# One instruction or four for each background matmul: the form chosen by the pace at which TensorE's code is fetched

## The chip, the cores and the metric

The kernel runs on one core of one Trainium2 chip. The metric is the time of one execution on the device in microseconds (us); lower is better. Below, PE is TensorE, ACT is ScalarE, DVE is VectorE, POOL is GpSimd, and SP is the engine that issues the DMAs.

## The reference

One transformer layer in bfloat16 on 2048 tokens of width 1024, with 32 heads of 32 and a hidden width of 3584:

```python
x = A_x                                        # 1 x 2048 x 1024
qkv = layernorm(x) @ wqkv                      # 1024 x 3072
p = softmax(q @ k.T * 32 ** -0.5)              # per head, 2048 x 2048
h = x + (p @ v) @ wo                           # 1024 x 1024
g = gelu(layernorm(h) @ w1 + b1)               # 1024 x 3584
out = h + g @ w2 + b2                          # 3584 x 1024
```

## The kernel before

The whole layer is one static program. A planner in Python (`Graph`) holds every step as a task with an engine, an estimated duration `occ`, a latency and its dependencies. `schedule` (line 113) plays the five engines forward in time and so fixes each engine's order; `assign` (line 255) turns the dependencies between engines into semaphore waits; `emit` (line 348) writes each engine's list out. Nothing is decided at run time: each engine runs its list in order and stops at a wait that has not come true.

**Attention** goes by queries: eight blocks of 256 queries, and in each block eight groups of four heads. A round takes 256 keys of one group. Its score matmuls (line 838) use the 128x128 array as four row strips, one head to a strip (mode "row"), and fill two units of PSUM; ACT takes the exponential of each unit (line 850). Then come the weighted sums of V (line 879) and the sums of the exponentials (line 918, with DVE adding pairs first at line 894); both use the array as four column strips of 32 (mode "col"). The last two groups of the last query blocks are done in halves of 128 queries. There are three PSUM units for scores, so PE can be at most one and a half rounds ahead of ACT.

**Background work** is everything else that is a matmul: the projections to Q, K and V, the output projection, and the two matmuls of the feed-forward part of earlier query blocks. `pick_pe` (line 1327) prefers scores whenever their PSUM is free, then weighted sums, then background, so background matmuls fill the gaps between attention's groups in PE's list. The planner charges 0.104 us each time PE goes from one mode to another.

A background matmul computes a 128-wide result block from 128 rows. In `mm` (line 588) it gets two forms, the same arithmetic into the same PSUM bank: a list of four matmuls of 128x32, one for each column strip, mode "col" (issued at line 596), or `whole`, one matmul of 128x128, mode "full" (issued at line 599). Each matmul that the kernel writes becomes two instructions of PE, a weight load and the matmul, and each wait of a task beyond the first is an instruction of its own. Some tasks have the one form only (line 602, and transposes at line 669): they are mode "full" from the start and `whole` is not set.

All background tasks with two forms are planned as "col". After planning, `merge_tiles` (line 240) changes some of them to "full": in a run of consecutive "col" tasks, a stretch of background work at its end becomes "full" if the run holds nothing else, or if the stretch takes at least 3.0 us.

Of the kernel before, what the change touches and what calls it, by code (L numbers as in the profile page):

```python
# [16 lines left out]

BULK = {1: 3, 2: 2}
UNIT = 1 << 19


class Buf:
# [42 lines left out]
class Graph:  # L65
# [47 lines left out]
    def schedule(self, pick_pe, pool, switch=0.104, dma_rate=280.0, dma_lat=2.1, dma_issue=0.06):  # L113
# [14 lines left out]
        def behind(t):  # L128
            k = BULK[t.prio] - t.bytes // UNIT
            for b in reversed(bulk):  # L130
                k -= b.bytes // UNIT
                if k < 0:
                    return b
            return None
# [20 lines left out]
        while n < total:  # L155
# [5 lines left out]
            for e in self.ENGS:  # L161
                while free[e] <= now + 1e-9:
# [8 lines left out]
                    else:  # L171
                        go = rd
                        if e == E.SP:
                            go = []
                            for x in rd:
                                b = behind(x) if x.bytes >= UNIT and x.prio in BULK else None
                                if b is None or b.done <= now + 1e-9:
# [27 lines left out]
                    if e == E.SP:  # L205
                        if t.bytes >= UNIT and t.prio in BULK:
                            b = behind(t)
# [10 lines left out]
                        s0 = max(state["dma"], start + 0.9)  # L218
                        state["dma"] = s0 + t.bytes / (330.0 if t.bytes >= UNIT and t.prio in BULK else dma_rate) / 1e3
                        t.done = max(state["dma"], s0) + dma_lat - 0.9  # L220
# [16 lines left out]
        return seqs  # L237


    def merge_tiles(self):  # L240

        run = []
        for t in self.seqs[E.PE] + [None]:
            if t is not None and t.mode == "col":
                run.append(t)
                continue
            k = len(run)
            while k and run[k - 1].whole is not None:
                k -= 1
            if k == 0 or sum(x.occ for x in run[k:]) >= 3.0:  # L250
                for x in run[k:]:
                    x.fns, x.mode = [x.whole], "full"
            run = []

    def assign(self, flows, lane_flows):

# [102 lines left out]
def build_kernel(nc, A_x, A_wqkv, A_wo, B_w1, B_b1, B_w2, B_b2, out):  # L359
    _, S, D = A_x.shape  # L360
# [16 lines left out]
    gr = Graph(N_LANES)  # L377
# [795 lines left out]
    for hc in range(8):  # L1173
# [7 lines left out]
        for k, r in [(k, hc) for k in range(min(hc, NLJ))] + ([(hc, r) for r in range(hc + 1)] if hc < NLJ else []):  # L1181
            n = 8 * k + r
            s = NR + 15 if n == 0 else n - 1 if n < 9 else n
# [174 lines left out]

    num = {t: i for i, t in enumerate(gr.tasks)}
    gr.schedule(pick_pe, pool_banks)  # L1360
    gr.merge_tiles()

    sems = {e: nc.alloc_semaphore(f"f_{e.name}") for e in (E.PE, E.Activation, E.DVE, E.Pool)}
    lanes = [nc.alloc_semaphore(f"f_lane{i}") for i in range(N_LANES)]
    gr.assign(sems, lanes)
    finals = [(("L", t.lane), t.value) for t in gr.seqs[E.SP][-40:]]

    with nc.Block() as block:
# [24 lines left out]
def bass_sequential_preLN__softmax_full_mha__dense_activation_gelu__prompt_kernel(  # L1393
    nc: bass.Bass,
    A_x: bass.AP,
    A_wqkv: bass.AP,
    A_wo: bass.AP,
    B_x: bass.AP,
    B_w1: bass.AP,
    B_b1: bass.AP,  # L1400
    B_w2: bass.AP,
    B_b2: bass.AP,
    out: bass.AP,
):
    build_kernel(nc, A_x, A_wqkv, A_wo, B_w1, B_b1, B_w2, B_b2, out)
# [28 lines left out]
```

## Time and profile before

| What | Value |
|---|---|
| Median of 3 timed runs | 1076.15 us (1075.17 to 1078.43) |
| Profiled execution's own time | 1076.72 us |
| Its span, first to last instruction | 1075.1 us |
| Granted TensorE clock, mean over the span | 0.998 |
| ACT busy | 1007.9 us (94%) |
| PE busy (ends of matmuls are modelled) | 1043.5 us (97%) |
| Matmuls on PE | 17,978 |
| DMA traffic, mean | 179 GB/s |

The profile is of one execution, and its span is 1.6 us shorter than that execution's own time. "Idle before" and "waits" name what ended an engine's idle time; "issue" there means that nothing which the profile shows was waited for. PEld is the weight load, which runs beside PE's matmuls. q8 is the DMA queue by which PE's instructions come, and PEclk is the granted share of TensorE's clock.

### The profile page before, as it was taken

The numbers are of one execution on the slowest core, as the hardware profiler recorded it, in microseconds if no ns is written. First come the engines' busy times: TensorE is split into PE (matmuls) and PEld (weight loads), VectorE is DVE, ScalarE is ACT, GpSimd is POOL, SyncE is SP. The second block draws the span as 40 slices with busy tenths as digits, with TensorE's granted clock in tenths as the row PEclk, the third lists the DMA queues.
The fourth block names the chain that finished last, engine by engine and source line by source line (L and its number), as shares of the span: only waits on it lengthen the run. The fifth ranks groups of instructions, "written<-read, shape, count | busy, mean of one in ns | idle before, by whom it ended". The sixth has DMA issues, their size and how long they took to land.

```text
span 1075.1 us, 39701 instructions
## 1 busy us (share of the span) xinstructions
PE 1043.5 (97%) x17978; PEld 605.1 (56%) x17978; DVE 783.2 (73%) x1521; ACT 1007.9 (94%) x1117; POOL 49.3 (5%) x110
## 2 busy tenths in 40 slices
PE   8999999999999999999999999999999899998998
PEld 6576555554445744664574456447546644663575
DVE  8766666566677995797599569749978967997560
ACT  4999999999999999999999989999999999999732
POOL 4200000000000010001001000100010000000000
PEclk9999999999999999999999999999999999999999
DMA  8470544335665546746554664657377453677730
GB/s 233 114 185 21 176 134 119 120 119 163 208 195 161 194 155 205 268 165 204 204 206 160 208 232 162 207 186 229 137 229 250 145 191 118 231 256 262 244 131 16
DMA packets 130649, 192.04 MB, mean 179 GB/s; under 512 B 47024, under 2 KB 95024, under 8 KB 127920
## 3 DMA queue, kind: packets, MB, share of 16 engines
q1 hardware_dynamic: 130480, 189.50, 54.2%
q8 instruction: 141, 2.31, 0.8%
q14 instruction: 28, 0.23, 0.1%
HBM read 175.32 MB, written 26.21 MB: 187 GB/s over the span
## 4 chain that ended last, share of the span: by engine, by line
PE 50%; ACT 41%; DMA 3%; DVE 3%; issue 1%; POOL 1%; SPq 0%; DVEq 0%
ACT PT L850 37%; PE ps L599 24%; PE ps L838 8%; PE ps L596 6%; PE ps L879 6%; PE ps L602 3%; PE ps L918 3%; ACT uu L1069 2%; ACT PX L850 2%; DMA a_w2r<-w_blocks 1%; DVE PS L894 1%; DMA w1b<-w_blocks 1%; DMA q_scratch<-lq 1%; DVE st L648 1%; DMA xrb<-in_A_x_dram 0%
## 5 line engine op out<-in xcount | busy, mean ns | idle before, releaser
L850 ACT ACTIVATE PT<-ps 128x1024 bf16<-128x1024 f32 x992 | 925.3, 1188 | 12.1 <-PE ps L838 11.7
L894 DVE TENSOR_TENSOR PS<-PT 128x1024 bf16<-128x1024 bf16 x427 | 280.1, 684 | 77.2 <-PE ps L918 40.3
L838 PE MATMUL ps<-QT,KT 32*128 32x256 bf16 (+1 forms) x4352 | 204.3, 266 | 10.4 <-ACT PT L850 6.8
L879 PE MATMUL ps<-PT,V 128*32 128x256 bf16 (+1 forms) x4224 | 160.4, 267 | 1.8 <-ACT PT L850 1.8
L838 PEld LDWEIGHTS ps<-QT,KT 32*128 32x128 bf16 x4352 | 64.6, 92 | 166.4 <-ACT PT L850 152.6
L599 PE MATMUL ps<-a_w2r,gT 128*128 128x512 bf16 x609 | 152.2, 381 | 3.2 <-DVE gT L1071 1.5
L599 PE MATMUL ps<-hnT,a_w1r 128*128 128x256 bf16 x1165 | 144.3, 275 | 0.6 <-DVE hnT L678 0.4
L599 PEld LDWEIGHTS ps<-hnT,a_w1r 128*128 128x128 bf16 x1165 | 107.8, 98 | 31.7 <-issue 18.2
L879 PEld LDWEIGHTS ps<-PT,V 128*32 128x32 bf16 x4224 | 101.3, 97 | 25.0 <-issue 7.6
L918 PE MATMUL ps<-PS,ones 128*32 128x256 bf16 (+1 forms) x1692 | 108.6, 268 | 1.0 <-DVE PS L894 0.8
L599 PEld LDWEIGHTS ps<-a_w2r,gT 128*128 128x128 bf16 x609 | 52.1, 98 | 73.7 <-issue 16.6
L1051 DVE TENSOR_TENSOR gT<-ps,b1f 128x512 bf16<-128x512 f32 x98 | 67.3, 687 | 22.1 <-PE ps L596 10.9
L599 PE MATMUL ps<-xnT,Wall 128*128 128x512 bf16 (+1 forms) x364 | 79.9, 355 | 0.4 <-ACT xnT L676 0.3
L1069 ACT ACTIVATE uu<-uu 128x1024 bf16<-128x1024 bf16 (+1 forms) x53 | 62.5, 1199 | 13.4 <-DVE uu L1068 13.4
L1124 DVE SCALAR_TENSOR_TENSOR hch<-ps,hch 128x512 bf16<-128x512 f32 x32 | 21.9, 685 | 71.2 <-PE ps L599 37.5
L596 PE MATMUL ps<-hnT,a_w1r 128*32 128x256 bf16 x1612 | 61.1, 274 | 6.3 <-issue 5.8
L599 PE MATMUL ps<-wov,OT 128*128 128x512 bf16 x224 | 56.0, 380 | 0.0
L918 PEld LDWEIGHTS ps<-PS,ones 128*32 128x32 bf16 x1692 | 42.9, 96 | 18.5 <-issue 6.3
L653 POOL CAST mvb<-mv 128x2 bf16<-128x2 f32 (+1 forms) x25 | 6.4, 254 | 984.6 <-DVE mv L650 984.6
L596 PE MATMUL ps<-a_w2r,gT 128*32 128x512 bf16 x700 | 50.2, 381 | 0.0
L599 PEld LDWEIGHTS ps<-xnT,Wall 128*128 128x128 bf16 x364 | 31.2, 97 | 33.0 <-issue 10.4
L596 PEld LDWEIGHTS ps<-hnT,a_w1r 128*32 128x32 bf16 x1612 | 40.8, 96 | 15.6 <-issue 13.9
(102 smaller groups left out, 992.6 us busy)
## 6 DMA issues: line engine op xcount, KB each, us to landing
a_w2r<-w_blocks SPq DMA_DIRECT2D x105, 512.0 KB, 4.6
a_w1r<-w_blocks SPq DMA_DIRECT2D x98, 512.0 KB, 3.9
wov<-wo_blocks SPq DMA_DIRECT2D x16, 1024.0 KB, 4.8
w_blocks<-in_B_w_dram SPq DMA_DIRECT2D x28, 512.0 KB, 3.9
w1b<-w_blocks SPq DMA_DIRECT2D x14, 512.0 KB, 4.2
Wall<-in_A_wqkv_dram SPq DMA_DIRECT2D x17, 256.0 KB, 4.5
xrb<-in_A_x_dram SPq DMA_DIRECT2D x16, 256.0 KB, 4.9
a_w1r<-in_A_wqkv_dram SPq DMA_DIRECT2D x8, 512.0 KB, 5.0
```

Of the source, the lines that this page charges most:

```text
L596: fns.append(lambda p, j=j: p.matmul(psum[32 * j:32 * j + 32, bi(bank), c0:c1], lhsT[:, 32 * j:32 * j + 32], rhs, start=start, stop=stop, ...
L599: t.whole = lambda p: p.matmul(psum[:, bi(bank), c0:c1], lhsT, rhs, start=start, stop=stop, skip_group_check=True)
L602: t = pe(lambda p: p.matmul(psum[:, bi(bank), c0:c1], lhsT, rhs, start=start, stop=stop), occ, reads=reads, writes=[bb(bank)], mode="full" ...
L648: dve(lambda v, c=c, k=k, x_ap=x_ap: v.bn_stats(st_l[:, i + k, 6 * c:6 * c + 6], x_ap[:, 512 * c:512 * c + 512]), 0.595, reads=B_x if isin ...
L838: return p.matmul(psum[:, 2 * us[h // 2] + h % 2, n * i:n * i + n], KT[32 * h:32 * h + 32, g, k0:k0 + P], QT[32 * h:32 * h + 32, qs, q0:q0 ...
L850: act(lambda a, u=u, k=k: a.activation(PTs[s][:, k, :, :], psum[:, 2 * u:2 * u + 2, :], ACT.Exp, bias=0.0, scale=SCALE), 1024, reads=[B_ps ...
L879: fns.append(lambda p, i=i, h=h: p.matmul(psum[32 * h:32 * h + 32, bi(bank), 0:nq], V[:, g, kt * r + i, 32 * h:32 * h + 32], PTs[s][:, h / ...
L894: dve(lambda v: v.tensor_tensor(PS[:, n, :, :], pairs[:, :, 0:256], pairs[:, :, 256:512], ALU.add), c_dve(1024, 2), reads=B_PTs[s], writes ...
L918: fns.append(lambda p, h=h, rhs=rhs, i=i: p.matmul(psum[32 * h:32 * h + 32, bi(bank), 256:256 + nq], ones32[:, :], rhs, start=False, stop= ...
L1051: t = dve(lambda v: v.tensor_tensor(g[:, fc:fc + nf, :], psum[:, bi(bank), :].rearrange("p (f c) -> p f c", f=nf), b1f[:, fc:fc + nf].unsq ...
L1069: act(lambda a: a.activation(w, w, ACT.Tanh, bias=0.0, scale=KT2), m, reads=[B_uu[i]], writes=[B_uu[i]], prio=-1)
L1124: drop(dve(lambda v: v.scalar_tensor_tensor(hch[:, hs, c], psum[:, bi(bank), :], half, hch[:, hs, c], ALU.mult, ALU.add), c_dve_ps(512), r ...
```

## The change

`merge_tiles` is replaced by `choose_forms`, which runs after `assign` instead of before it, when each task's waits are known. PE's list is cut into parts: stretches of background tasks with two forms, and stretches of everything else. For each stretch with two forms it picks one form for the whole stretch. To choose, it walks through PE's list counting instruction places (two for each matmul, one for each wait beyond the first), each with the planner's time. Places 192, 448, 704 and so on, every 256, are marks. If less time passes between two marks than a fetch takes, the difference is added to a price; `FETCH` lists ten fetch times, and the price is the mean over them. A stretch in full form pays 0.104 more for each side on which it meets other "col" work. The walk keeps the cheapest way to each position within a block (at most about 700 states) and takes the cheapest at the end.

The planner, the order of every engine and the waits are not touched.

```diff
+FETCH = (2.05, 2.55, 2.75, 3.0, 3.2, 3.45, 3.75, 4.15, 4.65, 5.75)
...
-    def merge_tiles(self):
-
+    def choose_forms(self, block=256, at=192, switch=0.104, weight=1.0):
+
+        parts = []
         run = []
         for t in self.seqs[E.PE] + [None]:
             if t is not None and t.mode == "col":
                 run.append(t)
                 continue
-            k = len(run)
-            while k and run[k - 1].whole is not None:
-                k -= 1
-            if k == 0 or sum(x.occ for x in run[k:]) >= 3.0:
-                for x in run[k:]:
-                    x.fns, x.mode = [x.whole], "full"
+            k = 0
+            while k < len(run):
+                n = k
+                while n < len(run) and (run[n].whole is None) == (run[k].whole is None):
+                    n += 1
+                ends = (k > 0) + (n < len(run))
+                parts.append((run[k:n], None if run[k].whole is None else switch * ends))
+                k = n
             run = []
+            if t is not None:
+                parts.append(([t], None))
+
+        def walk(ts, full):
+            marks, c = [], 0
+            for t in ts:
+                n = 1 if full else len(t.fns)
+                s = t.done - t.occ - t.lat
+                for w in t.waits[1:]:
+                    marks.append(s)
+                for i in range(n):
+                    marks += [s + t.occ * i / n, s + t.occ * (i + 1) / n]
+            return marks
+
+        states = {(2, 0): (0.0, 0.0, None)}
+        for p, (ts, extra) in enumerate(parts):
+            forms = [(False, 0.0)] if extra is None else [(True, extra), (False, 0.0)]
+            forms = [(f, x, walk(ts, f)) for f, x in forms]
+            new = {}
+            for (c, _), (price, t0, back) in states.items():
+                for f, x, marks in forms:
+                    y, s0 = price + x, t0
+                    k = (at - c) % block
+                    while k < len(marks):
+                        y += weight * sum(max(0.0, l - marks[k] + s0) for l in FETCH) / len(FETCH)
+                        s0 = marks[k]
+                        k += block
...
+        price, _, back = min(states.values(), key=lambda x: x[0])
+        self.fetch_price = price
+        while back is not None:
+            p, f, back = back
+            if f:
+                for t in parts[p][0]:
+                    t.fns, t.mode = [t.whole], "full"
...
     gr.schedule(pick_pe, pool_banks)
-    gr.merge_tiles()
...
     gr.assign(sems, lanes)
+    gr.choose_forms()
```

## Prediction, made before the changed kernel was run

> **What bounds the kernel now.** The page comes first.
>
> ```profile
> PE 1043.5 (97%) x17978; PEld 605.1 (56%) x17978; DVE 783.2 (73%) x1521; ACT 1007.9 (94%) x1117; POOL 49.3 (5%) x110
> q8 instruction: 141, 2.31, 0.8%
> PE 50%; ACT 41%; DMA 3%; DVE 3%; issue 1%; POOL 1%; SPq 0%; DVEq 0%
> ```
>
> ACT, with 992 exponentials, and PE share the chain. The q8 line matters here. PE has 17,978 weight loads, as many matmuls, and 138 others (waits that need an instruction of their own, two drains): 36,094. The 2.31 MB of q8 are 64 bytes for each, its 141 packets of 16 KB hold 256 each, 36,096 in all. So q8 is PE's own code, fetched while it runs.
>
> Second view, the waits: those of ACT from 80 us, where all is under way, to 990 us, near attention's end; those of ACT from 600 to 660 and from 850 to 885 us; and PE's weight loads (PEld) from 80 to 1005 us:
>
> ```profile
> ACT PT L850 <- PE ps L838: 7.3, 8, 2.4
> ...
> ACT PT L850 <- PE ps L838: 4.6, 3, 2.4
> ...
> ACT PT L850 <- PE ps L838: 2.0, 3, 1.0
> ...
> PEld ps L838 <- ACT PT L850: 146.7, 442, 1.9
> ```
>
> Over 910 us ACT waits 7.3 us for the scores (L838), 4.6 of it between 600 and 660 and 2.0 between 850 and 885. Elsewhere it is full, and in 442 of 512 groups the scores' weight loads wait for ACT: here a microsecond of ACT idleness is a microsecond of the end. Third view, the chain in order of time around the largest idle time, with ACT's rows of the timeline and the granted clock below it:
>
> ```profile
> 629.92 0.44 PE ps L596 x16
> 630.35 2.61 issue
> 632.97 0.51 PE ps L596 x12
> 633.48 0.41 PE ps L838 x8
> 633.89 2.89 PE ps L599 x13
> ...
> 637.23 1.53 PE ps L599 x13
> 638.76 0.33 PE ps L838 x8
> ...
> 643.56 1.53 PE ps L596 x52
> ...
> 645.97 0.33 PE ps L838 x8
> ```
>
> ```profile
> 633.93 1.94 ACT L850 ACTIVATE PT<-ps 128x1024 bf16<-128x1024 f32 x2 [2.40 <-PE ps L838]
> 637.29 2.87 ACT L850 ACTIVATE PT<-ps 128x1024 bf16<-128x1024 f32 x3 [1.42 <-PE ps L838]
> ```
>
> ```profile
> 634.00:635.00 1.00, 1.00 (x6) 0.74 (x5) 0.00 (x0) 1.00 (x2) 0.00 (x0) 0.50 0.27 102
> 635.00:636.00 1.00, 1.00 (x7) 0.69 (x6) 0.26 (x1) 0.87 (x1) 0.00 (x0) 0.50 0.02 8
> 636.00:637.00 1.00, 1.00 (x12) 0.37 (x10) 1.00 (x3) 0.00 (x0) 0.00 (x0) 0.50 0.26 98
> ```
>
> PE stops for 2.61 us inside a run of narrow matmuls, waiting for nothing the profile shows. Numbering PE's instructions (two per matmul, one per second wait), it stops at place 197 of a block of 256. The packet records show a q8 packet from 630.58 to 631.52; PE goes on 1.45 us after it. PE has five more such stops: 0.75 us at 648, 0.40 at 762, 2.07 at 856, 0.28 at 879, 1.10 at 1000. All are at places 196 to 200, 1.3 to 1.5 us after the end of a packet; in all 7.2 us. From one block's place 196 until the next block can go on took, over 133 fetches, 2.4 us at the lowest tenth, 3.2 median, 4.7 at the highest tenth, 6.8 at most.
>
> The second ACT row shows what a long stop does next: the granted clock is 0.50 from 634 to 637 (the clock record: 3.41 us), 13 matmuls take 2.89 us instead of 1.53, and ACT loses another 1.42. The 2.07 us stop had no such echo.
>
> [...]
>
> **The change, part by part.**
>
> *Order and waits.* The five engines' tasks stand in the same order in both programs; choosing forms after the waits are assigned moves no task and adds no wait and no data DMA. Cost nothing: nothing is moved past a queue.
>
> *Forms.* Of 4,482 background matmuls 482 go from one instruction to four (61 stretches) and 145 the other way (12 stretches); the matmuls become 18,989 (+1,011), and fetches 149 (+8, 0.13 MB beside 192 MB). A narrow task costs what a full one does: the chain shows 1.53 us for x13 full and 1.53 us for x52 narrow, of the same 256 columns. So form changes the instruction rate, not PE's time: 13 tasks are 26 places or 104.
>
> *Edges.* A scores group (L838) takes 0.33 us of chain before either form, 0.22 of it its own work. Start to start, entering full costs 105 ns and narrow 103, leaving full 96 and narrow 106: about 8 ns for each of 52 more narrow visits, 0.4 us. Mode changes rise from 1,030 to 1,050, at 0.1 us each 2.0 us. PE's addition is thus 2.4 us. On the path it is 0 if every one falls where PE is ahead of ACT, 2.4 if none does. I take 0.5, nearer to 0: the 442 waits of the scores' weight loads say that PE is mostly ahead, and only the edges added beside attention's own narrow work near 550 to 640 and 840 to 870 fall in rounds that PE fills.
>
> *Blocks.* I laid the trace's times of the same work, stops taken out, under both orders and cut at place 196 of each 256. Blocks under 4.0 us: 18 before, 3 after; under 4.5: 31 and 6; under 5.0: 42 and 7; under 6.0: 58 and 36. With the 133 measured fetch times for every block, the mean stop sums to 8.4 us before (7.2 were seen) and 3.0 after.
>
> *Sum*, against the profiled execution's own 1076.72 us (0.57 above the median of the three timed runs, inside their range):
> - the stops before 990 us go: 4.6 + 2.0 = -6.6. The 0.40 us stop at 762 is left out, since PE then waits 0.59 us for ACT anyway. If the 0.98 us ACT wait at 861, behind a DVE addition, is not the stop's, -5.6.
> - the block near 990 us (2.1 us; scores and weighted sums of 128 columns, which have one form) stays. Its stop was 1.10, its mean 1.3: +0.2 (0 at a fetch of 3.2, +1.5 at 4.7).
> - five blocks of 3.6 to 4.3 us stay, at 61, 65, 875, 879 and 1005 us: means 0.18, 0.12, 0.13, 0.14, 0.28; the last had 0.2 before: +0.6.
> - all other blocks together: 3.0 - 1.3 - 0.85 = +0.8.
> - edges: +0.5.
>
> -6.6 + 0.2 + 0.6 + 0.8 + 0.5 = -4.5: **1072.2 us**. With the unknowns at their good ends (no stop but the one near 990, no edges) 1070.1; at their bad ends (-5.6, +1.5, 1.4 doubled, edges 2.4) 1077.8, though they will hardly come together. The median may lie 0.6 lower than a profiled time, as it does before.
>
> **Rivals.**
> *Half the gain.* Fetches lengthen with traffic: the 6.8 us one began with 1.8 MB of loads under way, and the correlation of fetch time with bytes under way is 0.48. The 36 blocks under 6 us have room for 5 us but not for the tail. If every fetch took 4.5 us, six blocks would stop for 4.8 us in all, 1.8 more than the mean: 1074. One long stop near 990 us, over 2.4, could also halve the clock for 3.4 us where PE sets the pace: 1.7 more. Together 1074 to 1076.
>
> *No effect.* The fetch may be hidden, and the stops something else. Then only edges are left: 1076.72 + 0.5 = 1077.2, at most 1079.1. Against it: six stops out of six at the same place of a block and the same time after a packet. [...] The trace has blocks issued in 2.1 us against a median fetch of 3.2.
>
> *Slower: the cuts fall elsewhere.* The forms fit one alignment. With the list of fetch times in the change, its own sum of stops is 12.3 us before and 3.2 after; cut 32 places further 6.2, 64 places 10.9, 128 places 13.3. If the changed program's blocks start some 64 places or more from where they are counted, nothing is saved: 13.3 x 7.2/12.3 = 7.8 us of stops against 7.2, edges 0.5 and more stops long enough for the half clock (1.4): about 1079.2. Against it: counted the same way, before's stops drift only from 196 to 200 over 36,094 places, and 8 places off costs 0.4 us.
>
> **How the numbers follow.** Forecast 0.62, half the gain 0.25, no effect 0.07, elsewhere 0.06. From the median of 1076.15, 0.3% (about what a measurement of this kernel can tell from no change) is 3.2 us: faster means under 1072.9, slower over 1079.4. Of the forecast's case some 0.53 lies under 1072.9, and a little of half the gain; the rest of these two and no effect lie within; of the last a good half lies above. Faster 0.55, within 0.41, slower 0.04. The range of 8 in 10 takes the forecast and most of half the gain: 1069.6 to 1076.0.
>
> **What would show it.** q8 with 149 packets; 18,989 matmuls; ACT's wait for L838 between 80 and 990 us down from 7.3 to between 1 and 3 us, no piece over 1.5; one stop of 1 to 2 us near 990 to 1000; no stretch at half clock there. Wrong would be: issue stops over 0.5 us at other places between 80 and 980, ACT waits for L838 in many pieces of 0.1 us (edges), or the same stops at places far from 196.

## The result and the profile after

The changed kernel takes 1071.27 us (median of 13 runs, 1068.81 to 1074.43), the kernel before 1076.15 (13 runs beside them, 1073.86 to 1080.76): a ratio of 0.9957, 95% interval 0.9942 to 0.9972. By medians that is 4.9 us less. The profiled execution of the changed kernel took 1074.06 us, at the slow end of its runs and only 2.7 us less than the profiled execution of before. These two differences have to be explained apart.

First the page of the changed kernel: the engines, PE's code queue, and the share of each engine in the chain that ended last.

```profile
PE 1044.9 (97%) x18989; PEld 605.5 (56%) x18989; DVE 783.0 (73%) x1521; ACT 1007.7 (94%) x1117; POOL 49.2 (5%) x110
q8 instruction: 149, 2.44, 0.9%
ACT 72%; PE 21%; DMA 5%; DVE 1%; issue 0%; POOL 0%; SPq 0%; DVEq 0%
```

1,011 matmuls and 8 packets of code more, the same work on ACT. PE's share of the chain fell from 50% to 21%, ACT's rose from 41% to 72%: PE keeps ACT waiting in fewer places. Next the waits of the changed kernel (waited for: us in total, times, longest): ACT's from 80 to 990 us, where L898 is the exponential and L886 the scores (L850 and L838 before), then those of PE's weight loads from 80 to 1005 us.

```profile
ACT PT L898 <- PE ps L886: 2.5, 4, 0.9
ACT PT L898 <- PE ps L927: 0.3, 1, 0.3
...
PEld ps L886 <- ACT PT L898: 148.8, 453, 1.8
```

ACT's wait for the scores is 2.5 us instead of 7.3. From 600 to 660 us and from 850 to 885 us, where before had 4.6 and 2.0, the same question returns no row. The scores' weight loads wait for ACT in 453 groups instead of 442. PE's own waits from 80 to 1005 us hold two "issue" rows (the third row is a wait for a load that is needed further down), and the chain in order of time (start, length, what) has both stops:

```profile
PE ps L886 <- issue: 1.1, 1, 1.1
...
PE ps L644 <- issue: 0.8, 1, 0.8
PE ps L647 <- DMA wov<-wo_blocks: 0.7, 1, 0.7
```

```profile
473.11 0.27 PE ps L644
473.38 0.77 issue
474.15 0.40 PE ps L644 x7
...
994.36 0.28 PE ps L886 x11
994.64 1.07 issue
995.71 0.28 PE ps L886 x5
```

Before had six such stops with 7.2 us (a seventh, of 0.18 us at 273, is not in the prediction's list); 1.84 us are left. Both are fetches: PE goes on 1.46 and 1.39 us after the end of a packet. Their place is sharper than the prediction had it. When PE's instructions are counted as the trace records them (weight loads, matmuls, and 138 waits and drains), the two stand at places 192 and 193 of a block of 256. So do the six of before, and all 115 stops of 0.15 us or more in the fourteen profiles of this document: the drift from 196 to 200 that the prediction saw came of its count.

Where the rest went shows when the same exponentials are laid beside each other. The changed kernel is 1.1 us behind at 630 us, since the stop at 473 and the wait for wov at 580 cost it 1.1 and 0.8. Then it is 1.7 us ahead at 634, 3.25 at 637, 4.1 at 649, 4.5 at 763 and 6.5 at 861. So the stops that went are worth 7.6 us here, one more than the 6.6 of the prediction; that 6.5 us ahead at 861 looks like the 6.6 is an accident of the earlier loss. Then it loses again: 1.3 us between 897 and 902 (half clock, last section), 0.6 at 957 (a DMA of a_w1r), and 2.1 at 1029. The last is a row of PE's waits from 1010 to 1045 us:

```profile
PE ps L647 <- DMA w1b<-w_blocks: 2.1, 1, 2.1
```

PE waited for the feed-forward weights of the last query block. Before had no such wait.

### The profile page after: what moved, and what is told of

It is laid out like the page before. It is cut to its first block, busy times and chain, and to the rows that moved or that the text cites. A ratio compares the mean times of both kernels' runs of the same rounds, so it can differ in the third digit from the quotient of the medians.

```text
span 1072.4 us, 41723 instructions
## 1 busy us (share of the span) xinstructions
PE 1044.9 (97%) x18989; PEld 605.5 (56%) x18989; DVE 783.0 (73%) x1521; ACT 1007.7 (94%) x1117; POOL 49.2 (5%) x110
## 4 chain that ended last, share of the span: by engine, by line
ACT 72%; PE 21%; DMA 5%; DVE 1%; issue 0%; POOL 0%; SPq 0%; DVEq 0%
ACT PT L898 67%; PE ps L647 7%; PE ps L644 3%; PE ps L650 3%; ACT uu L1117 3%; PE ps L886 3%; PE ps L927 2%; ACT PX L898 2%; DMA a_w2r<-w_blocks 1%; PE ps L966 1%; DMA w2b<-w_blocks 1%; DMA wov<-wo_blocks 1%; DMA a_w1r<-w_blocks 1%; DMA xrb<-in_A_x_dram 1%; DMA w1b<-w_blocks 0%
## 5 line engine op out<-in xcount | busy, mean ns | idle before, releaser
L898 ACT ACTIVATE PT<-ps 128x1024 bf16<-128x1024 f32 x992 | 926.0, 1191 | 7.2 <-PE ps L886 6.7
L886 PE MATMUL ps<-QT,KT 32*128 32x256 bf16 (+1 forms) x4352 | 203.9, 266 | 9.4 <-ACT PT L898 7.0
L886 PEld LDWEIGHTS ps<-QT,KT 32*128 32x128 bf16 x4352 | 64.3, 92 | 163.5 <-ACT PT L898 153.0
L647 PE MATMUL ps<-a_w2r,gT 128*128 128x512 bf16 x443 | 111.0, 381 | 1.4 <-DVE gT L1099 0.8
L644 PE MATMUL ps<-a_w2r,gT 128*32 128x512 bf16 x1364 | 92.8, 385 | 1.8 <-DVE gT L1119 1.5
L647 PEld LDWEIGHTS ps<-a_w2r,gT 128*128 128x128 bf16 x443 | 38.1, 98 | 52.3 <-issue 11.6
L647 PE MATMUL ps<-xnT,Wall 128*128 128x512 bf16 (+1 forms) x253 | 55.9, 356 | 0.3 <-ACT xnT L724 0.3
L644 PEld LDWEIGHTS ps<-a_w2r,gT 128*32 128x32 bf16 x1364 | 31.7, 96 | 34.2 <-issue 11.7
L647 PE MATMUL ps<-wov,OT 128*128 128x512 bf16 x199 | 49.7, 380 | 0.7 <-DMA wov<-wo_blocks 0.7
```

What stands on the lines that cost most here:

```text
L644: fns.append(lambda p, j=j: p.matmul(psum[32 * j:32 * j + 32, bi(bank), c0:c1], lhsT[:, 32 * j:32 * j + 32], rhs, start=start, stop=stop, ...
L647: t.whole = lambda p: p.matmul(psum[:, bi(bank), c0:c1], lhsT, rhs, start=start, stop=stop, skip_group_check=True)
L886: return p.matmul(psum[:, 2 * us[h // 2] + h % 2, n * i:n * i + n], KT[32 * h:32 * h + 32, g, k0:k0 + P], QT[32 * h:32 * h + 32, qs, q0:q0 ...
L898: act(lambda a, u=u, k=k: a.activation(PTs[s][:, k, :, :], psum[:, 2 * u:2 * u + 2, :], ACT.Exp, bias=0.0, scale=SCALE), 1024, reads=[B_ps ...
```

## The experiments

Theory: PE stops where the next 256 instructions have not arrived, and the chosen forms keep each block longer than the fetch. Rivals: the gain comes from the forms themselves (fewer or cheaper instructions in some place); the change trades one stop for another, so its gain is given back by a transfer; edges between modes cost what the fetch gave. "Before" is always the kernel before on the same chip; its median was 1076.15 to 1079.76 us on the chips used, so only ratios are compared. The ratio given is the recorded estimate from all runs with its 95% interval, not the quotient of the two medians beside it; the two differ by up to 0.0015.

**1. The same forms, other cuts.** 96 waits that have long come true, each one instruction of PE, are put ahead of the first background tasks from 20 us on. In `pad96` they come after the forms were chosen, so every later block is cut some 96 places earlier in the work (94 of the waits are in the trace as instructions of their own). In `pad96r` the forms are chosen with the waits already there. Both pay for the 96 waits.

```diff
+    def pad(self, n, lo=20.0):
+        for t in self.seqs[E.PE]:
...
+            extra = [(("E", E.Pool), 1), (("E", E.Pool), 2)][:1 if t.waits else 2]
+            t.waits = list(t.waits) + extra
+            n -= 1
...
     gr.choose_forms()
+    gr.pad(96)          # pad96; in pad96r this line stands ahead of choose_forms
```

> The forms of the changed kernel, untouched; after they are chosen, 96 waits that are already true are put before background tasks from 20 us on, each one instruction of PE, so every later cut of 256 falls 96 places elsewhere. Theory fetch (the gain is that no block of 256 runs faster than its fetch): the gain goes, 1076 to 1077 (ratio to before 0.998 to 1.003), stops for nothing at places counted with the 96 included (196 to 200), some 8 us of them in the mean instead of 2.8. Rival forms (the gain comes from the forms themselves, their number or their edges, wherever the cuts fall): as the changed kernel, ratio 0.9957. Rival luck of the clock (only the half-clock stretch of the profiled run went away): 0.9957 too.

> The control to pad96: the same 96 waits, put in before the forms are chosen, so that the choice counts them. 18,941 matmuls instead of 18,989. Theory fetch: the gain is back, 1071 to 1072 (ratio 0.995 to 0.997). Rival forms: the same as pad96. If the 96 waits cost time of their own, both kernels show it: up to 96 x 0.05 = 4.8 us if nothing hid them, 0 if the sequencer runs ahead.

Measured: `pad96` 1081.42 us against 1079.76, ratio 1.0017 (1.0004 to 1.0029); `pad96r` 1076.48, ratio 0.9968 (0.9954 to 0.9983). The same forms with other cuts lose the whole gain, and choosing again brings it back. ACT's waits for the scores (L897 here) and PE's issue rows, from 80 us as above, first of `pad96`:

```profile
ACT PT L909 <- PE ps L897: 6.3, 11, 1.1
...
PE ps L655 <- issue: 2.3, 5, 1.0
...
PE ps L938 <- issue: 1.5, 1, 1.5
...
PE ps L977 <- issue: 1.2, 2, 0.8
...
PE ps L897 <- issue: 1.2, 2, 1.0
```

and of `pad96r`:

```profile
ACT PT L909 <- PE ps L897: 3.8, 7, 0.9
...
PE ps L897 <- issue: 1.0, 1, 1.0
PE ps L977 <- issue: 0.5, 1, 0.5
PE ps L938 <- issue: 0.3, 1, 0.3
```

Ten stops against three. They lie on four lines; what they share is not the line but the place: counted in the order of `pad96` itself, they stand at places 192 and 193 of a block again. Two of them in its chain:

```profile
587.63 0.21 PE ps L655 x4
587.84 1.02 issue
588.86 0.62 PE ps L655 x8
...
823.43 0.21 PE ps L897 x2
823.65 1.00 issue
824.64 0.39 PE ps L897 x6
```

This refutes the rival of the forms themselves, and with it the prediction's rival of no effect: the gain hangs on where the cuts lie. The waits themselves are no rival, since `pad96r` has them too. Nor is the half clock, the other rival of the expectation: the record of `pad96r` shows none before its end and that of `pad96` none at all (mean clock 1.000 in both profiles), and they differ by 3.5 us, of which 2.5 are ACT's waits for the scores.

**2. How far off may the count be?** As `pad96`, with 16 and 48 waits, and the changed kernel once more beside them.

```diff
-    gr.pad(96)
+    gr.pad(16)          # pad16; pad(48) in pad48; nothing in after2
```

> The changed kernel once more, on the same chip as the next three and with a second profile. Ratio 0.9957 as before. The first profile had a 2.1 us wait for w1b at 1029 us and a half-clock stretch at 894 us: if they belong to the changed kernel they are here again; if they are a matter of the single execution, at least one of them is not.

> As pad96 with 16 waits: cuts 16 places off, which in the dense spots is 0.2 us of PE work. Theory fetch: next to nothing is lost (mean stops 3.1 us instead of 2.8), ratio 0.9955 to 0.997. Rival (the waits themselves cost, so that pad96's loss was theirs): a sixth of pad96's loss, which is as small; pad48 tells.

> As pad96 with 48 waits. Theory fetch: about half of the gain is lost, mean stops 5.0 us: ratio 0.997 to 0.9995, between pad16 and pad96 (1.0017). Rival (the waits themselves): 0.9957 plus half of the 0.006 that pad96 lost, 0.9987, but then pad96r, with 96 waits, should have lost it too (it had 0.9968).

Measured, before 1079.09 us: `after2` 1075.9, ratio 0.9965 (0.9948 to 0.9982); `pad16` 1074.09, 0.9952 (0.9935 to 0.9969); `pad48` 1078.43, 0.999 (0.9976 to 1.0004). With 96 places at 1.0017 that is a curve: 16 places off cost nothing that can be measured, 48 most of the gain, 96 all of it. Of the two things that its expectation asks about, `after2` has one: its clock is halved again near 895 us (0.96 granted from 892 to 896 us, 0.50 from 896 to 899), where ACT waits 0.9 us for the scores, and there is no wait for w1b. So the half clock near 895 is of the changed kernel, though not in every execution (`w1bp1` below, with the same forms, has none). `pad48` has no control with forms chosen again, and its profiled execution shows only three stops, 1.4 us together, between 80 and 990 us; its loss agrees with the curve, and its own rows do not account for it.

**3. No full form at all.** Every background matmul with two forms as four instructions.

```diff
-    gr.choose_forms()
```

> All background matmuls that have two forms are left narrow (27,086 matmuls instead of 18,989, 1,061 mode changes instead of 1,050). Theory fetch: blocks of 3.5 us of PE work against a median fetch of 3.2 and a highest tenth of 4.7; many small stops, 26 us of them in all, the end about 18 us later than before (1087 to 1099; ratio 1.010 to 1.021). Rival forms: x52 narrow took what x13 full took, and there are 31 more mode changes than before, so at most 3 us later (ratio up to 1.003).

Measured: 1132.68 us, ratio 1.0479 (1.0458 to 1.05), far above what either theory gave. The page and the waits from 80 us:

```profile
PE 1064.5 (94%) x27086; PEld 634.8 (56%) x27086; DVE 785.8 (69%) x1521; ACT 1014.2 (90%) x1117; POOL 49.2 (4%) x110
q8 instruction: 212, 3.47, 1.3%
```

```profile
ACT PT L898 <- PE ps L886: 27.5, 37, 2.4
...
PE ps L644 <- issue: 16.6, 26, 2.2
```

and the chain at its end, where background work stands alone:

```profile
1060.18 1.97 PE ps L644 x128
1062.15 2.60 issue
1064.74 2.48 PE ps L644 x128
1067.23 2.36 issue
1069.59 5.44 PE ps L644 x253
1075.03 1.98 issue
1077.01 1.97 PE ps L644 x127
1078.98 2.27 issue
1081.24 1.97 PE ps L644 x128
1083.21 2.28 issue
```

This is the mechanism at its plainest: 128 matmuls are 256 instructions, they take 1.97 us, and then PE stops for 2.0 to 2.6 us. From 1060.18 to 1085.49 six blocks pass, one in 4.2 us in the mean, half clock included (0.74 granted from 1060 to 1073 us); the last two, at full clock (1.00 from 1073 to 1086 us), take 4.24 us each (the piece of x253 holds two, with no stop shown between them and a long one ahead of and behind them). In all there are 44 stops with 39.3 us between 80 us and the end, and the mean clock of 0.991 over the span of 1131.1 us is some 20 us at half clock, by estimate 10 us of lost work. The expectation of the theory was too low because the fetch time in it was (below), and because it left the half clock out.

**4. No narrow form at all.** Every background task with two forms as one instruction per matmul.

```diff
-    gr.choose_forms()
+    for t in gr.seqs[E.PE]:
+        if t.whole is not None:
+            t.fns, t.mode = [t.whole], "full"
```

> All background matmuls with two forms are full (15,638 matmuls, 1,309 mode changes instead of 1,050). Theory fetch with edges: stops as few as in the changed kernel, but 259 more mode changes at 0.1 us are 26 us of PE, about half of which reaches the end: 13 to 17 us later than before (1088 to 1094; ratio 1.010 to 1.016). Rival (fewer instructions are always better, edges are hidden since PE is ahead of ACT): as the changed kernel or better, ratio 0.993 to 0.996.

Measured: 1092.95 us, ratio 1.0132 (1.0107 to 1.0157), as expected. Of this kernel the page, with the chain by engine, and ACT's waits from 80 to 990 us:

```profile
PE 1065.4 (98%) x15638; PEld 588.2 (54%) x15638; DVE 787.7 (72%) x1521; ACT 1016.9 (93%) x1117; POOL 49.1 (5%) x110
q8 instruction: 122, 2.00, 0.7%
PE 86%; ACT 8%; DMA 2%; DVE 2%; issue 1%; POOL 0%; SPq 0%; DVEq 0%
```

```profile
ACT PT L898 <- PE ps L886: 7.8, 26, 0.8
```

Fetch stops between 80 and 1005 us are down to one of 0.8 us (another of 2.0 us follows at 1013; the mean clock of this profile is 0.998), and the kernel is slower: it has 1,309 mode changes instead of 1,050, which at 0.1 us each would be 26 us. PE's busy time is 20.5 us above the changed kernel's, 0.08 us for each, and PE has 86% of the chain. ACT's 7.8 us come in 26 pieces, none over 0.8. That is what edges look like here, and why fewest instructions is not the answer in this kernel either.

**5. The change in two parts.** `partA` makes only the 61 stretches narrow, `partB` only the 12 stretches full. On the same chip, a third theory was tested: that the gain is partly given back to the late w1b load of the profiled execution. `w1bp1` is the changed kernel with these loads at a better priority, `before_w1bp1` the kernel before with the same edit.

```diff
+    gr.base_forms()              # the forms of the old rule
     gr.choose_forms()
+    gr.mix_forms(True)           # partA: full if both say full; partB (False): if either does
```

```diff
-            dma(h[:, :, :], ..., writes=[b], prio=2, after=w1_loads[10:11])
+            dma(h[:, :, :], ..., writes=[b], prio=1, after=w1_loads[10:11])
```

> One part alone: the 61 stretches that the change makes narrow, without the 12 that it makes full (19,424 matmuls, 1,039 mode changes). Theory fetch: the forms only fit together; with 12 stretches left as they were, the cuts after the first of them (at 148 us) fall elsewhere, and the mean stops are those of before or more (9 us): ratio 1.000 to 1.004. Rival parts (each stretch brings its own share of the gain): the larger part, 61 of 73 stretches, brings most of it, 0.996 to 0.998.

> The other part alone: the 12 stretches that become full, without the 61 that become narrow (17,543 matmuls, 1,041 mode changes). Theory fetch: 12 spots of dense narrow work are gone, but no cut is placed: stops of 5.8 us in the mean, 1.6 less than before: ratio 0.998 to 1.001. Rival parts: 0.998 to 0.999 if it brings the rest. Rival full is better (fewer instructions): 0.996.

> The changed kernel with the late loads of w1b given the priority of the w2b loads, so that the last of them is issued six loads earlier; PE's order and forms are the same. Theory given back: in the changed kernel PE comes to that block earlier than its load lands (2.1 us of wait at 1029 us in the profiled run), so this wait goes, and with it 0 to 2 us: ratio to before 0.994 to 0.9955, no wait of PE for w1b. Rival chance: that wait was a slow load of one run, and the ratio stays at 0.9957; or another load of the same chain comes late instead (w2b, ratio 0.9957 to 0.997).

> The same priority in the kernel before, whose profile has no wait for w1b. Theory given back: nothing to gain, ratio 0.999 to 1.001. Rival (the order of these loads is worth something by itself): as much as w1bp1 gains over the changed kernel, 0.998.

Measured, before 1076.37 us: `partA` 1080.76, ratio 1.0046 (1.003 to 1.0062); `partB` 1073.84, 0.9991 (0.9975 to 1.0008); `w1bp1` 1071.5, 0.9959 (0.9938 to 0.9981); `before_w1bp1` 1076.91, 1.0008 (0.9994 to 1.0022).

`partA` is a little above what was expected of it (1.000 to 1.004). The interval of `partB` would still allow it half of the gain, but the parts do not add up: their product is 1.0037, and the whole with its forms untouched (`w1bp1`) has 0.9959 on this chip. ACT's waits from 80 to 990 us and PE's largest issue row of `partA`:

```profile
ACT PT L925 <- PE ps L913: 10.1, 9, 2.5
...
PE ps L671 <- issue: 6.7, 4, 2.7
```

Each of the 12 stretches that `partA` leaves narrow moves all later cuts by some 72 places (145 matmuls, six places each, in 12 stretches). That this makes the stops can be seen from the plan: eight of its ten stops from 80 us on come behind a block of 256 in which every background task has the form that it has in the changed kernel. So it is not narrow work too much in those spots, but cuts that lie elsewhere. The forms work as one list.

The earlier load brought nothing: `w1bp1` is where the change itself is. The wait for w1b was in none of the profiles of `after2`, `pad16`, `pad96` and `w1bp1`; `f10at` had 0.8 us of it. It is a matter of single executions, and belongs to the one that was profiled, not to the change.

**6. A better list of fetch times.** `FETCH` 1.0 us longer throughout, the marks at 197, where the prediction's count has the stops (the instructions in the trace have them at 192 and 193).

```diff
-FETCH = (2.05, 2.55, 2.75, 3.0, 3.2, 3.45, 3.75, 4.15, 4.65, 5.75)
+FETCH = (3.05, 3.55, 3.75, 4.0, 4.2, 4.45, 4.75, 5.15, 5.65, 6.75)
...
-    gr.choose_forms()
+    gr.choose_forms(at=197)
```

> A try at a better version: each of the ten fetch times of the choice 1.0 us longer, and the mark at place 197, where most stops were. 18,371 matmuls, 1,062 mode changes. The ready places then hold blocks of 5 us too short, so more room is made for slow fetches, at 12 more mode changes. Theory fetch: mean stops 2.3 instead of 2.8 us, edges 0.9 more: as the changed kernel within 0.1% (0.995 to 0.9965), with a smaller spread of the runs. Rival: the long fetches cost more than counted, and it is better by 0.2% (0.9935).

Measured: 1074.36 us against 1079.09, ratio 0.9957 (0.9937 to 0.9977), beside `after2` at 0.9965 on the same chip. The smaller spread that was expected did not come: its runs lie from 1070.57 to 1083.35 us, those of `after2` from 1072.9 to 1079.79. Not one stop of 0.15 us or more was left between 80 and 990 us in its profile, and still it is no faster than the changed kernel beyond doubt: what the changed kernel has left of stops there is little beside waits such as the 2.8 us for a_w2r in this profile.

## Why the prediction was right, step by step

**The cause** held: fetches that a block is too short for. The two largest stops went, and the gain goes and comes with the cuts (experiment 1); all that was forecast of the page came (149 packets, 18,989 matmuls), ACT's wait fell to 2.5 us with no piece over 1.5, and one stop of 1.07 us stands at 994.64.

**The half clock** did not go. The prediction took the 1.42 us behind the 2.61 us stop as saved for good. But 15 of 33 runs of the changed forms (`w1bp1` among them) have a mean clock of 0.998 or less, as one or more stretches at half clock give (one of 3.41 us takes 0.0016 off the mean over 1075 us), against 43 of 77 runs of before on the chips of the experiments. Among runs whose mean clock is 1.000 the gain is still there: 4.1 us between the means on the chip of experiment 5 (18 runs of before, 6 of `w1bp1`), 3.0 on that of experiment 2 (11 and 4 of `after2`). So most of the gain is the stops alone, and that the whole -6.6 came was in part luck. The 2.4 us from which a stop could halve the clock, in the rival of half the gain, was the author's estimate: before has a stop of 2.07 us without a half clock behind it and one of 2.61 with, `narrow` one of 2.27 without and one of 2.28 with (last section).

**The size** held by the medians: -4.5 us forecast, -4.9 measured, with an interval of 3.0 to 6.2; `after2` gives 0.9965 on another chip, 3.8 us. The profiled pair shows -2.7. Split at the start of the last exponential, ACT's idle time from 60 us on fell from 9.00 to 4.14 us, which is -4.9, and the rest of the span grew by 2.3, of which the wait for w1b is 2.1. Other profiles of the same forms have 5.80 (`after2`) and 1.93 us (`w1bp1`) of ACT idle time: single executions differ by as much as the change is worth, and the profile alone would have looked like the rival of half the gain. Before is no different: `before_w1bp1`, the forms of before with one load earlier, has 6.70 us of it where the profile that the prediction was read from has 9.00, and behind the last exponential it takes 62.6 us (`after2`: 62.5, without a wait for w1b) where that profile has 60.5. The mean of the two profiles of before less that of the three of the changed forms is 3.9 us.

**The terms.** The stops before 990 us: -6.6 forecast, 7.6 gained between 630 and 861 us. The 0.98 us wait at 861, of which the prediction was not sure, went with the stop, and the 0.40 us stop at 762, which it left out, was worth 0.7. The block near 990: 1.07 against 1.10, forecast +0.2. The five short blocks: +0.6 forecast, no stop of 0.15 us or more seen at any of them. The other blocks: +0.8 forecast, one stop of 0.77 seen. That one was named as a sign of a wrong prediction (over 0.5 between 80 and 980); it is read as one more draw from the fetch times (median 3.2 us, 6.8 at most by the prediction's count), not as another mechanism, since its place and its delay behind the packet are those of the others. Not in the sum were a stretch at half clock without any stop (0.92 us of ACT's wait, last section) and waits for DMAs, four of 0.3 to 2.1 us in this profile. That a sum which missed these came out near the medians, though the stops were worth more and the short blocks less than forecast, is partly luck.

**The mis-sized term: the fetch.** The prediction put it at 2.4, 3.2 and 4.7 us (lowest tenth, median, highest tenth), from all blocks, where the moment at which PE's instruction stream crosses a cut is not in the trace and was taken from the work at that place. After a stop it can be taken as the moment at which PE goes on. Over the 115 stops of all the profiles, the next packet starts 1.05 us or more (median 1.5) after PE goes on and ends 2.6 us after (median); PE goes on 1.2 to 1.6 us behind the end of a packet (median 1.43, once 0.75). The sums of the two, an estimate of the fetch, are 3.4 us at least, 4.1 in the median, 5.6 at the highest tenth and 7.0 at most. With that, the 4.2 us a block of `narrow` are what one has to expect, and its expectation of 1.010 to 1.021 was too low. In the change it mattered little, because most blocks had been kept well away: by the prediction's count 36 of them are under 6 us but only 7 under 5.

**Edges.** 0.5 us of the 2.4 possible was taken. No run here isolates it at that size; `allfull`, with 259 more of them, shows 0.08 us of PE's busy time for each where the prediction put 0.1.

**The rival "cuts elsewhere"** is real as a mechanism: it forecast 1079.2 for cuts 64 places off, 1.0028 of before, and `pad96` measured 1.0017. It didn't happen because the cuts lie where the change puts its marks: at 192, and the stops of all profiles stand at 192 and 193.

## What to carry to other kernels

The "issue" stops of PE that came at the same place of 256 instructions (192 or 193), 1.43 us in the median behind a packet of the instruction queue, are read here as the fetch of PE's own code: in `narrow` 128 matmuls of 1.97 us took 4.2 us a time, so their number set the pace of that row, not their own time. Before cutting instructions everywhere, price what the larger form costs (here 0.08 to 0.1 us for each change of how the array is split) and spend them where a block is short. An edit that adds or takes away instructions moves every later cut (96 more took the whole gain here), so such a list has to be made last and made again after each edit, and the parts of such a change can't be measured one by one. One profile of each kernel would have misled here: two executions of the same forms differ by as much as this change is worth.

## What the runs showed of the hardware

In these traces the half clock came behind some fetch stops, not behind others, and once without one. In before the granted clock is 0.50 for 3.41 us from 633.60 us, behind the stop of 2.61 us; behind the stop of 2.07 us, which ends at 856.44, it stays at 1.00. In `narrow` stops of 1.98, 2.27 and 2.28 us lie between 1075 and 1086 us; the granted clock is 1.00 from 1073 to 1086 us and 0.57 from 1086 to 1090, so that the last of the three alone has a half clock behind it. The changed kernel has one without any fetch stop in the 14 us before it: 0.50 for 3.41 us from 894.60 us (in `after2` 0.50 from 896 to 899 us). PE's and ACT's busy time by the microsecond (PE, PEld, DVE, ACT, POOL, then the granted clock, the DMA share and GB/s):

```profile
892.00:893.00 1.00, 0.48 (x20) 0.23 (x12) 1.00 (x4) 1.00 (x2) 0.00 (x0) 1.00 0.02 4
893.00:894.00 1.00, 0.59 (x16) 0.12 (x8) 1.00 (x2) 1.00 (x2) 0.00 (x0) 1.00 0.07 23
894.00:895.00 1.00, 0.48 (x16) 0.26 (x16) 1.00 (x4) 1.00 (x2) 0.00 (x0) 0.80 0.60 227
895.00:896.00 1.00, 1.00 (x17) 0.41 (x12) 1.00 (x3) 1.00 (x2) 0.00 (x0) 0.50 0.09 29
896.00:897.00 1.00, 1.00 (x16) 0.14 (x8) 1.00 (x4) 0.32 (x1) 0.00 (x0) 0.50 0.00 0
```

ACT is full and PE has little to do until 894, the clock falls at 894.6, and at 896 PE is full with 16 matmuls a microsecond while ACT runs dry: 0.92 us of wait. PE was busy for 0.48, 0.59 and 0.48 of the three microseconds from 892 to 895, so none of them was idle. Neither a length of stop nor a share of busy time from which the clock falls is shown by these rows, and no experiment was made on it.
